# Layer 2's up projection as seven block products instead of eight, with its weights converted early and streamed from DRAM

## The chip, the cores and the metric

The kernel runs on one core of one Trainium2 chip. The metric is device time in microseconds (us). TensorE multiplies matrices into PSUM, VectorE and ScalarE work on SBUF and PSUM, GpSimd (POOL) on SBUF alone, and SyncE (SP) issues all DMA transfers from one queue.

## The reference

Attention with rotary embedding feeds two feed-forward layers. There are 4 x 8 heads of 576 positions by 64; the heads are put side by side, so that a token has 512 features and there are 2304 tokens.

```
x = attention(q, k, v)                     # 2304 x 512
h = x @ w_in;  x = (h - tanh(h)) @ w_out   # layer 1: 512 -> 2048 -> 512
h = x @ w2_in; out = (h * sigmoid(1.702 * h)) @ w2_out   # layer 2, same sizes
```

## The kernel before

Every float32 operand of a matmul is split into a high part (a cast to float32r) and a low part (the remainder), and a product is three matmuls: high by high, high by low, low by high. In the feed-forward layers the tokens lie in six blocks of 384 (`TB`, block number j), and the 2048 hidden features in 16 blocks of 128 (f). An *item* is one pair (j, f). Its `up` (L769, matmuls in `up_chunk`, L716) is 4 blocks of the 512 inputs times three, 12 matmuls of 384 columns. The activation (`act`, L775) follows: in layer 1 four ScalarE and five VectorE steps, in layer 2 a sigmoid on ScalarE (L780) and a product on VectorE (L782). `split` (L808) casts the result to `gh` on ScalarE and subtracts `gl` on GpSimd. `down` (L818) adds to the output: in layer 1 12 matmuls of 384 columns with the weights stationary, in layer 2 9 of 512 columns with the activations stationary. `y_out` (L831) copies the sums out of PSUM and `y_save` stores them, layer 1's to the DRAM tensors `ys`, from which layer 2 fetches its blocks (`x_fetch`, `x_split`). Layer 1 runs blocks 0 and 1 in turns of four f, then the other blocks one by one; layer 2 is 96 items more.

The weights come as 64-bit words. `Conv` loads a block (`load`), and ScalarE, GpSimd and VectorE build float32 numbers (`head`, `bits`), of which `high` and `low` make the two parts. All 16 blocks of a layer stay in SBUF, in slabs of 128 x 4 x 512 (`wpa`, `wpc`, `wpb`). Layer 2's blocks are converted as layer 1's last items free the slabs.

The order on each engine is fixed ahead by `Plan`: each step has a priority, a cost and the tiles that it holds, and the planner picks, engine by engine, the step of the lowest priority number among those that could start about first. Priorities count from a nominal clock, `T(i)`, 4.16 us an item; the planner's own clock may run later than it. PSUM has four named banks (b0 and b1 hold `up` sums, b2 a layer 1 intermediate, b3 a conversion) and four for `down` sums.

Of the kernel before, what the change touches and what calls it, by code (L numbers as in the profile page):

```python
# [21 lines left out]
HP = H // 2  # L22
# [1007 lines left out]
```

## Time and profile before

| | |
|---|---|
| median of 3 runs | 1093.43 us (1093.26 to 1094.11) |
| profiled execution, span from first to last instruction | 1090.6 us |
| what the median has beyond that span | 2.8 us |
| TensorE busy, matmul instructions | 1067.2 us, 6272 |
| VectorE, ScalarE, GpSimd busy | 647.5, 670.1, 597.1 us |

The profiled execution's own time is recorded as that span alone. A matmul's duration overlaps the next one's, so the time between starts, not the duration, is what one more matmul costs.

### The profile page before, as it was taken

To read this page: it belongs to the slowest core of one execution; us is meant where nothing else is said; L and a number is where in the kernel's file an instruction comes from. 1 tells how busy PE (TensorE), PEld (TensorE's weight loads), DVE (VectorE), ACT (ScalarE), POOL (GpSimd) and SP (SyncE) were. 2 spreads that over 40 slices of the span, in tenths; PEclk is the share of its full clock that TensorE was granted. 3 is DMA by queue.
4 is the path that set the end of the run, shared out by engine and by line. 5 is a ranking of instruction groups with operands and counts; after the bars stand their busy time and mean duration, and the time that the engine had idled before them with its cause. 6 is when DMAs were issued, how large, how long until landed. Compare 5 with 4: busy or idle time off the path is not lost.

```text
span 1090.6 us, 17801 instructions
## 1 busy us (share of the span) xinstructions
PE 1067.2 (98%) x6272; PEld 1006.6 (92%) x6272; DVE 647.5 (59%) x1154; ACT 670.1 (61%) x1486; POOL 597.1 (55%) x502
## 2 busy tenths in 40 slices
PE   5999999999999999999999999999999999999998
PEld 4899999998999999999999999999999999999997
DVE  7899999989889987656667589544212111111111
ACT  5999999999887766566575678654322232232322
POOL 2888999986556677254262377767433232332221
PEclk9999999999999999999999999999999999999999
DMA  8777887777523324112031134543101010000000
GB/s 289 276 244 272 286 299 270 258 252 236 154 80 111 105 87 126 34 31 86 2 110 56 44 94 134 157 133 97 59 14 45 1 59 1 16 29 1 30 1 29
DMA packets 80778, 125.64 MB, mean 115 GB/s; under 512 B 9520, under 2 KB 50224, under 8 KB 80688
## 3 DMA queue, kind: packets, MB, share of 16 engines
q1 hardware_dynamic: 80688, 124.49, 34.9%
q8 instruction: 50, 0.82, 0.3%
q14 instruction: 40, 0.33, 0.1%
HBM read 77.20 MB, written 18.95 MB: 88 GB/s over the span
## 4 chain that ended last, share of the span: by engine, by line
PE 80%; DVE 9%; ACT 5%; issue 2%; DMA 2%; POOL 1%; SPq 1%; ACTq 0%; POOLq 0%; DVEq 0%
PE ps_h L716 35%; PE y L829 35%; PE sp L441 4%; PE ps_o L520 3%; PE ps_e L478 2%; DVE mx L447 2%; ACT e L453 2%; DVE el L504 2%; ACT eh L506 1%; DMA qk<-in_qk_dram 1%; DVE cz L289 1%; DVE cz L287 1%; DVE eh L504 1%; PE ps_e L482 1%; POOL qk L364 0%
## 5 line engine op out<-in xcount | busy, mean ns | idle before, releaser
L716 PE MATMUL ps_h<-xh,w 128*128 128x384 f32 x1536 | 422.6, 336 | 0.6 <-DVE xt L529 0.6
L814 POOL TENSOR_TENSOR gl<-t,gh 128x384 fp32r<-128x384 f32 x192 | 194.9, 1016 | 366.6 <-ACT gh L812 358.0
L716 PEld LDWEIGHTS ps_h<-xh,w 128*128 128x128 f32 x1536 | 280.4, 188 | 5.3 <-DVE xt L529 0.8
L716 PE MATMUL ps_h<-xl,w 128*128 128x384 f32 x768 | 257.2, 335 | 0.0
L812 ACT CAST gh<-t 128x384 fp32r<-128x384 f32 x192 | 98.8, 514 | 196.1 <-PE y L829 93.3
L782 DVE TENSOR_TENSOR t<-t,ps_h 128x384 f32<-128x384 f32 x96 | 53.1, 553 | 268.9 <-ACT t L780 268.5
L829 PE MATMUL y<-gh,w 128*128 128x384 f32 x768 | 195.1, 334 | 0.8 <-ACT gh L812 0.8
L829 PE MATMUL y<-w,gh 128*128 128x512 f32 x576 | 179.2, 392 | 0.0
L716 PEld LDWEIGHTS ps_h<-xl,w 128*128 128x128 f32 x768 | 144.2, 188 | 4.1
L780 ACT ACTIVATE t<-ps_h 128x384 f32<-128x384 f32 x96 | 47.2, 492 | 161.8 <-PE ps_h L716 157.1
L829 PEld LDWEIGHTS y<-gh,w 128*128 128x128 f32 x768 | 138.6, 188 | 1.5 <-ACT gh L812 1.5
L829 PE MATMUL y<-gl,w 128*128 128x384 f32 x384 | 128.6, 335 | 1.0 <-POOL gl L814 0.9
L829 PEld LDWEIGHTS y<-w,gh 128*128 128x128 f32 x576 | 106.8, 188 | 17.8
L441 PE MATMUL sp<-kt,qt 128*128 128x288 f32 x624 | 114.3, 311 | 2.0 <-ACT e L453 1.1
L829 PE MATMUL y<-w,gl 128*128 128x512 f32 x288 | 113.9, 396 | 0.0
L453 ACT ACTIVATE e<-sp,mx 128x576 f32<-128x576 f32 x144 | 107.1, 745 | 7.4 <-DVE mx L447 6.3
L447 DVE TENSOR_REDUCE mx<-sp 128x1 f32<-128x576 f32 x144 | 106.6, 747 | 4.0 <-PE sp L441 2.6
L298 POOL TENSOR_TENSOR w<-cz,w 128x512 fp32r<-128x512 f32 x64 | 82.8, 1295 | 46.4 <-ACT w L294 44.7
L506 ACT CAST eh<-ps_e 128x512 fp32r<-128x512 f32 (+2 forms) x208 | 103.3, 527 | 5.3 <-PE ps_e L478 3.4
L504 DVE TENSOR_TENSOR el<-ps_e,eh 128x512 fp32r<-128x512 f32 x144 | 95.8, 684 | 4.9 <-ACT eh L506 3.8
L797 DVE SCALAR_TENSOR_TENSOR w<-z,ps_h 128x384 f32<-128x384 f32 x96 | 52.8, 550 | 76.3 <-ACT t L790 74.7
L441 PEld LDWEIGHTS sp<-kt,qt 128*128 128x128 f32 x624 | 87.9, 189 | 8.9 <-ACT e L453 7.9
(71 smaller groups left out, 1726.3 us busy)
## 6 DMA issues: line engine op xcount, KB each, us to landing
kt<-qk SPq DMA_DIRECT2D x64, 288.0 KB
qk<-in_qk_dram SPq DMA_DIRECT2D x30, 576.0 KB
st<-in_moe_w_in_dram SPq DMA_DIRECT2D x32, 512.0 KB
st<-in_moe_w_out_dram SPq DMA_DIRECT2D x32, 512.0 KB
qt<-qk SPq DMA_DIRECT2D x64, 144.0 KB
x<-xs SPq DMA_DIRECT2D x16, 384.0 KB
v<-in_v_dram SPq DMA_DIRECT2D x16, 320.0 KB
xs<-xt SPq DMA_DIRECT2D x16, 288.0 KB
```

The costliest lines, as they stand in the source:

```text
L298: nc.gpsimd.tensor_sub(w[:, 2 * self.half + 1], self.cz, w[:, 2 * self.half].bitcast(F32))
L441: nc.tensor.matmul(sp[:, half, 0:HS], lhsT=w, rhs=m[:, half * HS:(half + 1) * HS], start=(o == 0), stop=(o == len(ops) - 1))
L447: nc.vector.tensor_reduce(mx, st["sp", n, i], axis=AX.XY, op=ALU.max, negate=True)
L453: nc.scalar.activation(e.rearrange("p (a b) -> p a b", a=2), st.pop(("sp", n, i)), AF.Exp, bias=st.pop(("mx", n, i)), accum_out=st["sum", ...
L504: nc.vector.tensor_sub(lo, src, hi.bitcast(F32))
L506: nc.scalar.copy(hi, src)
L716: nc.tensor.matmul(p, lhsT=wi[:, a, kk, :], rhs=xx[:, kk, :], start=(o == 0), stop=(o == 11))
L782: nc.vector.tensor_mul(gt[i], gt[i], p)
L797: nc.vector.scalar_tensor_tensor(w, z, G_C[3], p, op0=ALU.mult, op1=ALU.mult)
L812: nc.scalar.copy(gs[i][0], g)
L814: nc.gpsimd.tensor_sub(gs[i][1], g, gs[i][0].bitcast(F32))
L829: nc.tensor.matmul(y, lhsT=lhs, rhs=rhs, start=first and o == 0, stop=last and o == 2)
```

## The change

In layer 2, two token blocks (the pair p) and two f blocks (fp and fp + 8) form a *quad*. The four `up` results of a quad are the blocks of a 2 x 2 block product, in which the 512 inputs are halved too. Instead of eight block products of 256 inputs, seven are formed (Strassen's scheme in Winograd's form), each of 6 matmuls of 384 columns, from sums of the weight blocks and of the token blocks. The results share partial sums: ScalarE copies product 1 into a second bank as the start of another sum (`seed`), sets two partial sums aside (`keep`), and VectorE adds them to the last sum (`join`). Seven operand tiles of a token pair are made by GpSimd subtractions and ScalarE casts (`mixed`, `operand`) from the raw blocks. The `down` matmuls are those of before; six sums of a pair stay open over its 8 quads, in the four `down` banks and b2 and b3. `h2` uses b0 and b1.

The weights of layer 2, with the sums of their blocks, are converted while layer 1 runs, split into high and low parts, and stored in DRAM (`w2`). Each quad loads its three slabs again (`w_load`). Layer 1's outputs of blocks 2 to 5 go through the row tiles `rb` and `rc`. In the diff, conversion steps (`word`) are those of `queue` before without `high` and `low`.

```diff
+C2, CU, CL = 34, 6, 25
...
+        if u[0] == "h2":
+            return BANKS[0:2]
+        if u[0] == "y2":
+            return TAGS["y"] + BANKS[2:4]
+        if u[0] == "ws":
+            return SLABS
+        if u[0] == "xo":
+            return ["xh.0", "xl.0", "xh.1", "xl.1"] + SLABS
+        if u[0] == "o":
+            return ["part.0", "part.1", "st.0", "st.1"]
+        if u[0] == "raw":
+            return TAGS["part"] if u[1] else SLABS
+        if u[0] == "yo":
+            return TAGS["rb"] + TAGS["rc"]
+        if u[0] in ALSO:
+            return [x for k in ALSO[u[0]] for x in TAGS[k]]
...
+    ALSO = {"su": ("z", "w"), "g2": ("t",), "g2h": ("gh", "mk"), "g2l": ("gl", "mk")}
+
...
+    SLABS = TAGS["wpa"] + TAGS["wpc"] + TAGS["wpb"]
...
+    w2 = [[dram.tile([128, 4, 512], F32, name=f"w2{s}{i}") for s in range(3)] for i in range(NF // 2)]
...
+    def pieces_of(src, wd, key, dst, reads, urgent, uses):
+        u = ("o",) + key
+
+        def high():
+            if u not in ot:
+                ot[u] = part_tile(u)
+            nc.scalar.copy(ot[u][:, 0:wd].bitcast(F32R), src())
+
+        def low():
+            nc.gpsimd.tensor_sub(ot[u][:, 512:512 + wd].bitcast(F32R), src(), ot[u][:, 0:wd])
+
+        def store():
+            nc.sync.dma_start(out=dst, in_=ot[u][:, 0:1024].rearrange("p (a f) -> p a f", a=2)[:, :, 0:wd])
+
+        f = wd / 512
+        op(urgent, high, [_cost("ACT", 0.23 + 0.38 * f)], reads, [("oh",) + key], [u] + uses)
+        op(urgent, low, [_cost("POOL", 0.18 + 1.12 * f)], reads + [("oh",) + key], [("ol",) + key], [u] + uses)
+        op(urgent, store, [("SP", 0.62, 1.6 * f)], [("oh",) + key, ("ol",) + key], [("w2",) + key], [u], dl=(1.2, 0.8))
+
+    def conv_in(fp, prio, urgent, after):
+        cs = [Conv((1, f), w2_in, w2_out, 0) for f in (fp, fp + NF // 2)]
+        ids = [c.word(prio + n, urgent + n, after) for n, c in enumerate(cs)]
+        cz = [("cz",) + i for i in ids]
...
+        S = [("S", fp, k) for k in range(4)]
+        K = [("in", fp, r) for r in range(4)]
+        pieces_of(lambda: cs[0].cz, 512, K[0], w2[fp][0][:, 0:2], [z[0]], t, cz)
+        pieces_of(lambda: a(1, 1), 256, K[3], w2[fp][1][:, 2].rearrange("p (a f) -> p a f", a=2), [z[1]], t, cz)
+        op(t, lambda: summed(0), cost, [z[1]], [S[0]], cz + [X])
+        op(t, lambda: summed(1), cost, [z[0], S[0]], [S[1]], cz + [X])
+        pieces_of(both, 512, K[1], w2[fp][0][:, 2:4], [S[0], S[1]], t, [X])
+        done = [("ol",) + K[1]]
+        op(t, lambda: summed(2), cost, z + done, [S[2]], cz + [X])
+        op(t, lambda: summed(3), cost, [z[0], S[1]] + done, [S[3]], cz + [X])
+        pieces_of(both, 512, K[2], w2[fp][1][:, 0:2], [S[2], S[3]], t, [X])
+
+    def conv_out(f, prio, urgent, after):
+        c = Conv((1, f), w2_in, w2_out, 1)
...
+        pieces_of(lambda: c.cz, 512, ("out", f), w2[fp][2][:, 2 * n:2 * n + 2], [("z",) + i], urgent + 1, [("cz",) + i])
...
+                P = ("yo", j, d) if j > 1 else ("part", j)
...
+    FP = NF // 2
+    for fp in range(FP):
+        t = T(C2 + CU * fp)
+        conv_in(fp, t, t + CL, t)
+        for n in range(2):
+            u = t + (0.5 + 0.25 * n) * CU * UN
+            conv_out(fp + FP * n, u, u + CL, u)
+
+
+    UQ = 15.7
+    NQ = 3 * FP
+    PROD = {1: (0, 0, 0), 6: (0, 2, 256), 2: (0, 0, 256), 5: (0, 2, 0), 7: (1, 0, 0), 3: (1, 0, 256), 4: (1, 2, 0)}
...
+    def w_load(q, s):
+        t = ws[q, s] = slab(("ws", q, s), "ws")
+        n = 3 if s == 1 else 4
+        nc.sync.dma_start(out=t[:, 0:n].bitcast(F32), in_=w2[q % FP][s][:, 0:n])
...
+    def mixed(p, k):
+        if k in (1, 3, 4):
+            xt2[p, k] = xp.tile([128, 2, TB], F32, tag=cur[0].slot["x", 1, p, k], name="x", bufs=1)
+        if k == 1:
+            nc.gpsimd.tensor_sub(xt2[p, 1], block(p, 0, 1), block(p, 0, 0))
+        elif k == 3:
+            nc.gpsimd.tensor_sub(xt2[p, 3], block(p, 1, 1), block(p, 0, 1))
+        elif k == 2:
+            nc.gpsimd.tensor_sub(block(p, 0, 1), block(p, 1, 1), xt2[p, 1])
+        else:
+            nc.gpsimd.tensor_sub(xt2[p, 4], block(p, 1, 0), block(p, 0, 1))
+
...
+    def operand(p, n, low):
+        a = source(p, n)
+        if not low:
+            xo[p, n] = slab(("xo", p, n), "xo")[:, :, 0:TB]
+            nc.scalar.copy(xo[p, n][:, 0:2], a)
+        else:
+            nc.gpsimd.tensor_sub(xo[p, n][:, 2:4], a, xo[p, n][:, 0:2].bitcast(F32))
+    made = [("w2", "in", fp, r) for fp in range(FP) for r in range(4)] + [("w2", "out", f) for f in range(NF)]
+
+    def x_ops(p):
+        t = T2(FP * p) - (30 if p else 5)
+        R = [("raw", p, h) for h in range(2)]
+        for h in range(2):
+            op(t - 4, lambda h=h: raw_load(p, h), [("SP", 0.62, 1.6)], [("ys", 2 * p + h, d) for d in range(NK)]
+               + ([("h0", FP * p - 5)] if p else made), [("raw", p, h)],
+               [R[h]], t - 14, dl=HBM)
+        X = {k: ("x", 1, p, k) for k in (1, 3, 4)}
+        XO = {n: ("xo", p, n) for n in PROD}
+        held = {1: [R[0]], 2: [R[0]], 3: [R[1]], 4: [X[4]], 5: [X[1]], 6: [R[1]], 7: [X[3]]}
+        got = {1: ("raw", p, 0), 2: ("raw", p, 0), 3: ("raw", p, 1), 4: ("T", p, 4), 5: ("T", p, 1), 6: ("T", p, 2), 7: ("T", p, 3)}
+        add = _cost("POOL", 1.86)
+        for k, reads, uses in ((1, [("raw", p, 0), ("raw", p, 1)], R + [X[1]]),
+                               (3, [("raw", p, 1)], [R[1], X[3]]),
+                               (2, [("T", p, 1), ("T", p, 3), ("raw", p, 1)], [R[1], X[1]]),
+                               (4, [("T", p, 2), ("raw", p, 0)], R + [X[4]])):
+            op(t + k * 0.01, lambda k=k: mixed(p, k), [add], reads, [("T", p, k)], uses)
+        for o, n in enumerate((1, 6, 2, 5, 7, 3, 4)):
+            for low in (False, True):
+                op(t + 2 * o, lambda n=n, low=low: operand(p, n, low), [add if low else _cost("ACT", 0.8)],
+                   [got[n]] + ([("xoh", p, n)] if low else []), [("xol" if low else "xoh", p, n)], held[n] + [XO[n]])
+
+    def product(q, n):
+        p = q // FP
+        s, a, o = PROD[n]
+        w, x = ws[q, s], xo[p, n]
+
...
+        b = {1: 0, 2: 0, 6: 1, 5: 1, 3: 1, 7: 2, 4: 2}[n]
+        if n in (1, 7):
+            hq[q, b] = bank(("h2", q, b), "ps_h")[:, 0:TB]
+        c = 0
+        for k in range(2):
+            for lw, lx in ((0, 0), (0, 1), (1, 0)):
+                nc.tensor.matmul(hq[q, b], lhsT=wt(lw, k), rhs=x[:, 2 * lx + k], start=n in (1, 7) and c == 0,
+                                 stop=n in (2, 3, 4) and c == 5, skip_group_check=True)
+                c += 1
+
+    def seed(q):
+        hq[q, 1] = bank(("h2", q, 1), "ps_h")[:, 0:TB]
+        nc.scalar.copy(hq[q, 1], hq[q, 0])
+
+    def keep(q, n):
+        su[q, n] = slab(("su", q, n), "su", F32)
+        nc.scalar.copy(su[q, n], hq[q, 1])
+
+    def join(q, n):
+        if n == 0:
+            su[q, 3] = slab(("su", q, 3), "su", F32)
+            nc.vector.tensor_add(su[q, 3], hq[q, 2], su[q, 4])
+        else:
+            nc.vector.tensor_add(hq[q, 2], hq[q, 2], su[q, 2])
+
...
+    def quad_ops(q):
+        p, fp = divmod(q, FP)
+        t = T2(q)
+        H = [("h2", q, b) for b in range(3)]
+        Ws = [("ws", q, s) for s in range(3)]
+        SU = {n: ("su", q, n) for n in (2, 3, 4)}
+        for s in range(3):
+            src = [("w2", "in", fp, 2 * s + r) for r in range(2)] if s < 2 else [("w2", "out", f) for f in (fp, fp + FP)]
+            op(t - 20 + 2 * s, lambda s=s: w_load(q, s), [("SP", 0.62, 4.0)], src + ([("h0", q - 2)] if q > 2 else []),
+               [("wsl", q, s)], [Ws[s]], t - 34, dl=HBM)
+
+        def pr(n, prio, reads, writes, b):
+            op(t + prio, lambda: product(q, n), [("PE", 1.04, 1.21)],
+               [("xoh", p, n), ("xol", p, n), ("wsl", q, PROD[n][0])] + reads, writes, [H[b], Ws[PROD[n][0]], ("xo", p, n)])
+
+        pr(1, 0, [("h2", q - 1)] if q else [], [("h0", q)], 0)
+        op(t + 1, lambda: seed(q), [_cost("ACT", 0.5)], [("h0", q)], [("h1", q)], [H[0], H[1]])
+        pr(2, 2, [], [("h0", q)], 0)
+        pr(6, 2.1, [], [("h1", q)], 1)
+        op(t + 3, lambda: keep(q, 2), [_cost("ACT", 0.5)], [("h1", q)], [("k2", q)], [H[1], SU[2]])
+        pr(5, 5, [], [("h1", q)], 1)
+        op(t + 6, lambda: keep(q, 4), [_cost("ACT", 0.5)], [("h1", q)], [("k4", q)], [H[1], SU[4]])
+        pr(3, 8, [], [("h1", q)], 1)
+        pr(7, 9, [], [("h2", q)], 2)
+        op(t + 10, lambda: join(q, 0), [_cost("DVE", 0.555)], [("h2", q), ("k4", q)], [("c3", q)], [H[2], SU[3], SU[4]])
+        op(t + 10, lambda: join(q, 1), [_cost("DVE", 0.555)], [("k2", q), ("c3", q)], [("h2", q)], [H[2], SU[2]])
+        pr(4, 12, [], [("h2", q)], 2)
+        for u, at, src, hold in ((0, 3, ("h0", q), H[0]), (1, 9, ("h1", q), H[1]), (3, 11, ("c3", q), SU[3]), (2, 13, ("h2", q), H[2])):
+            G, GH, GL = ("g2", q, u), ("g2h", q, u), ("g2l", q, u)
+            op(t + at, lambda u=u: act2(q, u, 0), [_cost("ACT", 0.62)], [src], [("a2", q, u)], [hold, G])
+            op(t + at + 1, lambda u=u: act2(q, u, 1), [_cost("DVE", 0.555)], [src, ("a2", q, u)], [("g", q, u)], [hold, G])
+            op(t + at + 2, lambda u=u: split2(q, u, 0), [_cost("ACT", 0.515)], [("g", q, u)], [("gh2", q, u)], [G, GH, GL])
+            op(t + at + 2, lambda u=u: split2(q, u, 1), [_cost("POOL", 1.01)], [("g", q, u), ("gh2", q, u)], [("gl2", q, u)], [G, GH, GL])
+            n, j = divmod(u, 2)
+            for c in range(3):
+                Y = ("y2", p, j, c)
+                op(t + at + 6 + c, lambda u=u, c=c: down2(q, u, c), [("PE", 0.693, 0.9)],
+                   [("gh2", q, u), ("gl2", q, u), ("wsl", q, 2)], [("yd2", p, j, c)], [GH, GL, Ws[2], Y])
...
+    for q in range(NQ):
+        if q % FP == 0:
+            x_ops(q // FP)
+        quad_ops(q)
```

## Rows read from the trace of the kernel before

**Rows 1.** The page: busy time by engine; granted clock and DMA rate in 40 slices.

```profile
PE 1067.2 (98%) x6272; PEld 1006.6 (92%) x6272; DVE 647.5 (59%) x1154; ACT 670.1 (61%) x1486; POOL 597.1 (55%) x502
...
PEclk9999999999999999999999999999999999999999
...
GB/s 289 276 244 272 286 299 270 258 252 236 154 80 111 105 87 126 34 31 86 2 110 56 44 94 134 157 133 97 59 14 45 1 59 1 16 29 1 30 1 29
```

**Rows 2.** The chain that ended last, layer 2: start us, us, what.

```profile
691.47 2.08 PE y L829 x9
...
1003.34 2.10 PE ps_h L716 x12
1005.45 2.08 PE y L829 x9
...
1080.81 6.18 PE y L829 x27
```

**Rows 3.** Stretches: length, busy us of PE, PEld, DVE, ACT, POOL, clock, DMA.

```profile
270.00:290.00 20.00, 18.79 (x128) 17.61 (x127) 17.42 (x32) 15.84 (x38) 8.46 (x10) 1.00 0.62 183
...
640.00:680.00 40.00, 40.00 (x232) 40.00 (x232) 37.26 (x67) 31.01 (x66) 26.57 (x27) 1.00 0.40 122
...
389.00:660.00 271.00, 270.17 (x1554) 268.92 (x1554) 189.29 (x355) 172.80 (x375) 133.86 (x135) 1.00 0.23 70
```

**Rows 4.** Timeline near the end: the last `up` matmul of an item, its sigmoid, its product.

```profile
1076.29 0.33 PE L716 MATMUL ps_h<-xh,w 128*128 128x384 f32 x1
...
1076.72 0.49 ACT L780 ACTIVATE t<-ps_h 128x384 f32<-128x384 f32 x1 [1.88 <-PE ps_h L716]
...
1077.24 0.55 DVE L782 TENSOR_TENSOR t<-t,ps_h 128x384 f32<-128x384 f32 x1 [3.63 <-ACT t L780]
```

**Rows 5.** Timeline of layer 1: a cast on ScalarE and the `down` that waited for it.

```profile
371.78 0.51 ACT L812 CAST gh<-t 128x384 fp32r<-128x384 f32 x1 [1.90 <-DVE t L805]
...
372.35 0.62 PE L829 MATMUL y<-gh,w 128*128 128x384 f32 x2 [0.48 <-ACT gh L812]
```

**Rows 6.** Groups by line and form: busy us, mean ns of one, then idle before.

```profile
L814 POOL TENSOR_TENSOR gl<-t,gh 128x384 fp32r<-128x384 f32 x192 | 194.9, 1016 | 366.6 <-ACT gh L812 358.0 <-ACT z L788 3.5 <-issue 2.6
...
L812 ACT CAST gh<-t 128x384 fp32r<-128x384 f32 x192 | 98.8, 514 | 196.1 <-PE y L829 93.3 <-DVE t L805 80.1 <-PE ps_h L716 17.4
...
L298 POOL TENSOR_TENSOR w<-cz,w 128x512 fp32r<-128x512 f32 x64 | 82.8, 1295 | 46.4 <-ACT w L294 44.7 <-DVE el L504 0.9 <-PE y L829 0.4
...
L364 POOL TENSOR_TENSOR qk<-qk,tab 128x1152 f32<-128x1152 f32 x28 | 74.4, 2668 | 5.9 <-PE ps_o L520 2.8 <-DMA xs<-xt 2.1 <-DMA st<-in_moe_w_out_dram 0.4
...
L782 DVE TENSOR_TENSOR t<-t,ps_h 128x384 f32<-128x384 f32 x96 | 53.1, 553 | 268.9 <-ACT t L780 268.5
...
L780 ACT ACTIVATE t<-ps_h 128x384 f32<-128x384 f32 x96 | 47.2, 492 | 161.8 <-PE ps_h L716 157.1 <-POOL gl L814 4.7
...
L287 DVE SCALAR_TENSOR_TENSOR cz<-cp,cz 128x512 int32<-128x512 int32 x64 | 43.7, 683 | 40.7 <-POOL cz L285 37.5 <-ACT cp L276 2.8
L285 POOL TENSOR_SCALAR cz<-st 128x512 int32<-128x512 uint8 x64 | 42.1, 658 | 5.5 <-DMA st<-in_moe_w_out_dram 0.2
...
L276 ACT ACTIVATE cp<-st 128x512 f32<-128x512 f32 x64 | 40.5, 632 | 0.0
...
L294 ACT CAST w<-cz 128x512 fp32r<-128x512 f32 x64 | 39.5, 620 | 12.3 <-DVE cz L289 11.6
...
L426 POOL TENSOR_TENSOR vw<-v,vw 128x640 fp32r<-128x640 f32 x16 | 25.5, 1593 | 4.9 <-PE sp L441 2.3 <-ACT vw L370 2.0
...
L370 ACT CAST qk<-qk 128x1152 fp32r<-128x1152 f32 x15 | 17.5, 1167 | 0.0
...
L838 ACT COPY part<-y 128x384 f32<-128x384 f32 x24 | 10.6, 482 | 0.2
...
L370 ACT CAST vw<-v 128x640 fp32r<-128x640 f32 x7 | 5.5, 792 | 0.0
```

**Rows 7.** Timeline of SP's queue at the end of layer 1.

```profile
688.87 1.91 SPq L846 DMA_DIRECT2D ys<-part  x4
```

More of the change, by code (lines that the diff above doesn't have):

```diff
@@ L806, in act, with split @@
             gt[i] = t
[L808 removed]
+    def split(i, k, names=("gh", "gl")):
         g = gt[i]
         if k == 0:
[L811 removed]
+            key = (i,) if isinstance(i, int) else i
+            gs[i] = [slab((t,) + key, t[-2:]) for t in names]
             nc.scalar.copy(gs[i][0], g)
@@ L842, in y_save @@
     def y_save(i, d):
-        mo, j = items[i][:2]
-        n = (TB, DM)[mo]
-        r = j * TB + d * 128
-        nc.sync.dma_start(out=out[r:r + 128, :] if mo else ys[j][d], in_=part[mo, j][:, d * n:(d + 1) * n])
+        j = items[i][0]
+        nc.sync.dma_start(out=ys[j][d], in_=part[j, d])
     UN = 4.16
@@ L915, in item_ops @@
+        for d in range(NK):
+            Y = ("y", d, j, lo_of[i])
+            w = 3 * 0.173
+            op(t + MD + 0.01 * d, lambda d=d: down(i, d), [("PE", w, w + 0.2)],
+               [("gh", i), ("gl", i)] + [(x, 0, f, 1) for x in ("wh", "wl")]
+               + (["down"] if i or d else []), [("yd", d, j, lo_of[i]), "down"], [GH, GL, Wt, Y])
             if last:
-                n = (TB, DM)[mo]
-                P = ("part", mo, j)
-                cost = _cost("ACT", 0.49 if n == TB else 0.59) if lo_of[i] == 0 else _cost("DVE", 0.547 if n == TB else 0.68)
@@ L936, in attention_moe_kernel @@
         item_ops(i)
-    for f in range(NF):
-        for half in range(2):
-            m = 2 * f + half
-            t = T(n1 - 10 + m if m < 10 else n1 + (m - 10) / 2)
-            Conv((1, f), w2_in, w2_out, half).queue(t - 6, t, max(0, t - 30))
-    for i in range(n1, 2 * n1):
-        for (mo, j), s in first_item.items():
-            if mo and s - 8 == i or (mo == 1 and i == n1 and s < n1 + 8):
-                fetch_ops(mo, j, T(s - 8))
-        item_ops(i)
+    FP = NF // 2
[5 more added lines that the diff above has]
+            conv_out(fp + FP * n, u, u + CL, u)
@@ new lines, in split2, with down2 @@
+    def split2(q, u, k):
+        g = gt[q, u]
+        if k == 0:
+            gs[q, u] = [slab((t, q, u), t[1:] if 0 else t) for t in ("g2h", "g2l")]
+            nc.scalar.copy(gs[q, u][0], g)
+        else:
+            nc.gpsimd.tensor_sub(gs[q, u][1], g, gs[q, u][0].bitcast(F32))
+    def down2(q, u, c):
+        p, fp = divmod(q, FP)
+        n, j = divmod(u, 2)
+        gh, gl = gs[q, u]
+        cols = slice(c * 128, (c + 1) * 128)
+        first, last = fp == 0 and n == 0, fp == FP - 1 and n == 1
+        if first:
+            acc["2", p, j, c] = bank(("y2", p, j, c), "y")
+        y = acc["2", p, j, c]
+        for o, (a, g) in enumerate(((0, gh), (1, gh), (0, gl))):
+            nc.tensor.matmul(y, lhsT=g[:, cols], rhs=ws[q, 2][:, 2 * n + a, :], start=first and o == 0, stop=last and o == 2)
```

296 lines of the change are left out of this document (174 added, 122 removed).

## Prediction

> **What bounds the kernel now.** I read the page first: TensorE is busy 98% of the span and its granted clock never falls, while DMA traffic in the second half is a small part of what the first half shows possible [rows 1]. "Busy" can hide waits, so next comes the chain of work that ended last: in layer 2 it is TensorE alone, 12 matmuls of `up` in 2.10 us, then 9 of `down` in 2.08 us, and again, and the end is three groups of `down` in a row [rows 2]. Then the stretches: in the second half of layer 1 (389 to 660 us) TensorE is busy 270.2 of 271 us, and even where the old conversions of layer 2's weights fill VectorE to 93% (640 to 680 us) TensorE loses nothing [rows 3]. So from there on the time is the number of matmuls times their pitch. Removing a matmul pays in full as long as no new wait takes its place; moving work off the other engines pays nothing by itself. The profiled execution has a span of 1090.6 us; the median of the runs is 1093.43, so about 2.8 us lie around the span, and I take them as unchanged.
>
> **What is removed.** Layer 2's `up` is 96 items of 12 matmuls, 1152. After the change it is 24 quads (two token blocks by two f blocks) of seven products of 6 matmuls, 1008. The `down` matmuls stay at 24 x 36 = 864, the same form. So 144 matmuls of 384 columns go. At the pitch of the row, 2.10/12 = 0.175 us, that is **-25.2 us**, or 1.05 us per quad [rows 2]. A quad then holds 42 x 0.175 + 36 x 2.08/9 = 7.35 + 8.32 = 15.67 us of TensorE.
>
> The Trainium skill ("TensorE: Matmul & The Clock Gate", section "Back-to-back issue gap") gives an isolated warm matmul of N columns N/2.4 + 2.5 ns, here 162.5 ns, by which 144 matmuls would be worth 23.4 us (an estimate from that page). The rows have 175 ns with the weight loads in between, and the measurement decides.
>
> **The new order inside a quad.** Before, an `up` only needed a free bank. Now TensorE's seven products depend on other engines, with two banks for three sums. The hops, from the rows: ScalarE starts 0.43 us after the last matmul of an `up` starts, which is 0.26 us after the slot in which the next matmul could start [rows 4]; a ScalarE copy of 128x384 out of PSUM takes 0.48 [rows 6]; TensorE starts 0.06 after ScalarE ends [rows 5]. So:
> - product 1 to `seed` to products 2 and 6: product 2 adds into the bank that `seed` reads, so it waits too, 0.26 + 0.48 + 0.06 = 0.80 us. The bank that `seed` writes comes free by the quad before: its product 4, then sigmoid, multiply and the copy, 0.26 + 0.49 + 0.03 + 0.55 + 0.03 + 0.48 + 0.06 = 1.90 us, of which the new product 1 covers 1.05. So 0.85 us at most are left.
> - product 6 to `keep` to product 5, and product 5 to `keep` to product 3: 0.80 us each.
> - product 7 to two `join` on VectorE (0.55 each, 0.03 between) to product 4: 0.26 + 1.13 + 0.06 = 1.45 us [rows 4, 6].
>
> Behind a waiting `seed` or `keep` on ScalarE stand sigmoids and `gh` casts, for which later `down` groups wait. What `down` work must cover is 0.85 + 0.80 + 0.80 + 1.45 = 3.9 us, and a quad has 12 groups of three `down` matmuls, 0.69 us each, 8.3 us. The groups are also ready in time: a block needs 0.26 + 0.49 + 0.55 + 0.51 + 1.02 and hops, about 3.1 us, from its last product to its `gl` [rows 4, 6], and three blocks of the quad before are waiting while this quad's chain runs. The closest fit is product 5 to product 3, where the priorities leave one group (0.69) against 0.80. Lower bound 0 per quad; upper bound 3.9, all hops bare. I take 0.15 us per quad, the one tight hop and a little queueing on ScalarE: **+3.6 us**. The other engines have room: per quad ScalarE 3 x 0.48 + 4 x (0.49 + 0.51), with an eighth of seven 768-wide copies (about 0.89, between the 640 and 1152 rows) and of six output copies, about 6.7 of 15.67 us; VectorE 6 x 0.55 = 3.3; GpSimd 4 x 1.02 and an eighth of eleven 768-wide subtractions of about 1.86 (between the 640 and 1152 rows), 6.6 us [rows 6].
>
> **The streamed weights.** A quad loads 1.05 + 0.79 + 1.05 = 2.88 MB in 15.67 us, 184 GB/s; the page has slices of 299 GB/s [rows 1], at which it takes 9.6 us. SP issues them in one queue with the x loads and the output stores, each waiting for a free slab; a load that waits holds up those behind it. Twenty slots serve: two operand sets of seven and one raw block fill 15 at the worst, around a change of token pair, and leave five. A set of three for the next quad can then go only as the last quad's slabs come free, about 20, 16 and 9 us before each is read. I cost it at nothing, hidden by that lead; if the lead is gone, 9.6 us at each of the two pair changes.
>
> **The conversions.** They leave the stretch where they cost TensorE nothing, so that gains nothing. They arrive in layer 1, by their load times from about 389 us. 32 words need VectorE 32 x 2 x 0.68, 44 us, as before; ScalarE 32 x 0.63 + 40 x 0.62 + 8 narrow copies, 48 us; GpSimd 32 x 0.66 + 40 x 1.30 + 40 of 256 columns at about 0.74 (extended from the 384 and 512 rows), 103 us, where it was 63 [rows 6]. Added to what 389 to 660 us already holds, an over-count since some old conversions lie in it, VectorE comes to 233, ScalarE 221 and GpSimd 236 of 271 us [rows 3]. That is full but under what 640 to 680 shows without loss. What can hurt is one conversion step ahead of a `gl` or an activation in an engine's queue, 0.6 to 1.3 us; TensorE then waits for `gl`. Lower bound 0 (640 to 680); upper bound the 270 to 290 stretch, 1.21 us lost of 20, which over 271 us is 16 us [rows 3]. I take **+1.5 us**, near the row of the same stage. The outputs of blocks 2 to 5 now share three row tiles, so the fourth copy waits for the first store; the four stores issue in 1.91 us [rows 7] and the next block's `down` needs that bank more than 4 us later, so nothing.
>
> **Opening of layer 2 and end.** The two raw x loads of the first pair wait for every stored piece, and then eleven 768-wide GpSimd steps (20.5 us, some 27 beside the `gl` steps) make the operands. The first nine `down` matmuls in layer 2's form start at 691.5 us, two items behind their `up` [rows 2], so layer 2 starts near 691.5 - 2.1 - 8.3 = 681 us; even conversions that end at 650 leave the first operands in time. Opening, pair changes and the tail together: **+0.8 us** (lower 0).
>
> Sum: 1090.6 - 25.2 + 3.6 + 1.5 + 0.8 = 1071.3 us of span, with 2.8 around it **1074 us**.
>
> **Rivals.**
> 1. The full gain: all hops and conversions hidden, 1068 to 1070. For it: the cover counts above. Against: the one tight hop and fuller queues. 0.14.
> 2. A jam in layer 1: conversions in front of `gl`. For: three engines above 80%, GpSimd with 40 us more. Against: 640 to 680. At the upper bound 1093.4 - 25.2 + 3.6 + 16.4 + 0.8 = 1089. 0.10.
> 3. Late data: the stores end only with layer 1, then loads of 1.6 MB (5.3 us) and 20.5 us of GpSimd against some 10 us of TensorE's work, 16 us lost, or slabs late at the pair changes, 19 us. 1088 to 1091. 0.10.
> 4. Slower: the hops inside a quad stay bare, because the fixed order puts `down` groups elsewhere or the other engines lag it. It decides at 1.05 us per quad, 27% of the 3.9 us; all bare gives 24 x 3.9 = 94 us, 1162. For: before, no matmul of `up` waited for a copy. Against: 8.3 us of cover for 3.9. 0.09, and 0.03 for other losses beyond 25 us.
> 5. No difference: losses happen to equal the gain, 0.04.
>
> The forecast, 1070 to 1079, has 0.50. **Numbers.** Faster by over 0.2% (2.2 us, about what a measurement of this kernel can tell from no change) 0.50 + 0.14 + 0.20 = 0.84; within 0.04; slower 0.12. The range from 1068 to 1089 leaves out the slower cases, the equal one and a little of rivals 1 to 3; the forecast's own range is 1070 to 1079.
>
> **What will show it.** Right: layer 2's stretch is about 376 + 4 us long and TensorE waits in it are a few tenths per quad, on product 3; layer 1 ends within 2 us of before. Wrong: waits on `keep`, `join` or `seed` above 1 us per quad (rival 4); waits of `down` on `gl` between 389 and 660 (2); a gap of TensorE near 681 us or at each eighth quad, ended by a DMA or by GpSimd's operand step (3).

## Result, and the profile after

The changed kernel takes **1076.87 us** (median of 4 runs, 1075.84 to 1079.64). The kernel before, run beside it, took 1093.35 us. That is 16.5 us less; the forecast was 1074 us, 19.3 us less. The recorded ratio is 0.9856 [0.9842, 0.9870]; it is not the quotient of the two medians, which is 0.9849 and lies inside the interval. The profiled execution took 1075.84 us with a span of 1074.0 us.

On the page, TensorE has 144 instructions fewer, and the granted clock does not fall. GpSimd has 74 us more to do, and the last part of the DMA row, almost empty in [rows 1], now carries the stream.

```profile
PE 1048.0 (98%) x6128; PEld 980.6 (91%) x6128; DVE 673.4 (63%) x1196; ACT 715.7 (67%) x1571; POOL 671.1 (62%) x559
...
PEclk9999999999999999999999999999999999999999
...
GB/s 284 279 239 295 262 274 315 241 264 247 158 100 91 106 97 210 185 175 206 208 201 239 174 301 314 83 378 118 69 150 338 191 209 132 215 347 251 108 1 59
```

**Where the 16.6 us of span went.** Two points divide both executions: the slot in which layer 1's own matmuls are done, and the end of the last `down`. In the kernel before, layer 1's last `down` and the `up` that follows it in TensorE's timeline are these:

```profile
689.05 0.33 PE L829 MATMUL y<-gl,w 128*128 128x384 f32 x1
689.23 0.33 PE L716 MATMUL ps_h<-xh,w 128*128 128x384 f32 x1
```

By 689.23 TensorE had already done two `up` items of layer 2 (24 matmuls, the second from 685.07 to 687.15, 2.08 us each). Without them layer 1 would have ended at 689.23 - 4.16 = 685.07. In the kernel after, 18 product matmuls, the first two rows, stand between layer 1's last `down` groups (L1119 is a product, L929 a `down` of layer 1; the last row is cut off where the view ends):

```profile
685.58 1.20 PE L1119 MATMUL ps_h<-xo,ws 128*128 128x384 f32 x6
...
688.70 2.24 PE L1119 MATMUL ps_h<-xo,ws 128*128 128x384 f32 x12
...
692.69 0.33 PE L929 MATMUL y<-gl,w 128*128 128x384 f32 x1
692.86 1.37 PE L1119 MATMUL ps_h<-xo,ws 128*128 128x384 f32 x7
```

Their slots are 1.04 and 2.08 us, so layer 1 would have ended at 692.86 - 3.12 = 689.74. The last 27 `down` matmuls close both chains, at 1080.81 + 6.18 before [rows 2] and here:

```profile
1064.02 6.17 PE y L1164 x27
```

| part | before | after | difference | forecast |
|---|---|---|---|---|
| attention, up to layer 1's first `up` | 286.31 | 286.60 | +0.3 | 0 |
| layer 1, to the points above | 398.8 | 403.1 | +4.4 | +1.5 |
| layer 2, to the end of the last `down` | 401.9 | 380.5 | -21.5 | -25.2 + 3.6 + 0.8 = -20.8 |
| last output copy and stores | 3.6 | 3.8 | +0.2 | in the 0.8 |
| span | 1090.6 | 1074.0 | -16.6 | -19.3 |

**A quad.** TensorE's products in the timeline, from product 5 of one quad to product 5 of the next. The pitch is 882.23 - 866.36 = 15.87 us; the working had 15.67 + 0.15 + a little.

```profile
866.36 1.23 PE L1119 MATMUL ps_h<-xo,ws 128*128 128x384 f32 x6
867.43 0.63 PE L1164 MATMUL y<-ws,g2h 128*128 128x512 f32 x2
867.89 0.40 PE L1164 MATMUL y<-ws,g2l 128*128 128x512 f32 x1
868.16 2.38 PE L1119 MATMUL ps_h<-xo,ws 128*128 128x384 f32 x12
...
882.23 1.23 PE L1119 MATMUL ps_h<-xo,ws 128*128 128x384 f32 x6
```

Product 5 (866.36) is followed by one `down` group, then by products 3 and 7 together. In between, ScalarE takes the copy `keep`, and its row in ScalarE's timeline ends at 868.10, 0.06 us before product 3 starts:

```profile
867.62 0.48 ACT L1129 COPY su<-ps_h 128x384 f32<-128x384 f32 x1 [2.94 <-PE ps_h L1119]
```

The weight loads' waits between 690 and 1074 us name this copy and, but for one `g2l` of 0.2 us, nothing else (us in total, times, longest):

```profile
PEld ps_h L1119 <- ACT su L1129: 6.8, 22, 0.3
```

**Layer 1.** The stretches that answer to [rows 3]. From 270 to 290 us, in attention, TensorE is busy 18.79 of 20 us as before. From 389 to 660 us VectorE has 27 us more, ScalarE 30, GpSimd 81, and TensorE is busy 2.85 us less:

```profile
389.00:660.00 271.00, 267.32 (x1527) 263.99 (x1527) 216.33 (x397) 202.36 (x430) 214.64 (x226) 1.00 0.63 212
```

It has also done 27 matmuls fewer there (1527 against 1554), which at 2.08/12 us each is 4.7 us. So a wait costs more than its idle time; the first matmul behind the wait at 590 us (last row of the second view below) takes 0.44 us instead of 0.33.

TensorE's largest waits within layer 1 (from 690 us on its matmuls show none):

```profile
PE y L929 <- POOL gl L916: 1.6, 4, 0.5
PE y L929 <- ACT yo L941: 1.3, 1, 1.3
PE ps_h L826 <- DVE t L900: 0.9, 2, 0.7
```

The third line is a conversion standing in an engine's queue. The rows of VectorE and of the matmul at 590 us: two conversion steps (L320, L322) go ahead of the activation (L898, L900), which ends at 590.08, and the bank comes free for TensorE then.

```profile
587.73 0.69 DVE L320 SCALAR_TENSOR_TENSOR cz<-cp,cz 128x512 int32<-128x512 int32 x1 [1.13 <-POOL cz L318]
588.46 0.69 DVE L322 SCALAR_TENSOR_TENSOR cz<-cp,cz 128x512 int32<-128x512 int32 x1
589.07 0.55 DVE L898 SCALAR_TENSOR_TENSOR w<-z,ps_h 128x384 f32<-128x384 f32 x1
589.53 0.55 DVE L900 TENSOR_TENSOR t<-ps_h,t 128x384 f32<-128x384 f32 x1
...
590.13 0.44 PE L826 MATMUL ps_h<-xh,w 128*128 128x384 f32 x1 [0.70 <-DVE t L900]
```

The second is an output block with three row tiles: three copies go at once, the fourth starts 6.6 us after them, and TensorE needs its bank. The stores of the first three tiles were issued by 627.2 us. From 627.2 us to the fourth copy ScalarE works through ten other steps, four of them conversion steps, with one gap of 0.26 us; so when the copy ran was set by the order on ScalarE at least as much as by the tile.

```profile
624.26 1.52 ACT L941 COPY yo<-y 128x384 f32<-128x384 f32 x3
...
632.41 0.47 ACT L941 COPY yo<-y 128x384 f32<-128x384 f32 x1
...
632.93 0.61 PE L929 MATMUL y<-gh,w 128*128 128x384 f32 x2 [1.29 <-ACT yo L941]
```

### The profile page after: what moved, and what is told of

It reads as the page before. It is cut to its first block, busy times and chain, and to the rows that moved or that the text cites. A ratio compares the mean times of both kernels' runs of the same rounds, so it can differ in the third digit from the quotient of the medians.

```text
span 1074.0 us, 17841 instructions
## 1 busy us (share of the span) xinstructions
PE 1048.0 (98%) x6128; PEld 980.6 (91%) x6128; DVE 673.4 (63%) x1196; ACT 715.7 (67%) x1571; POOL 671.1 (62%) x559
## 4 chain that ended last, share of the span: by engine, by line
PE 64%; DVE 14%; ACT 9%; POOL 5%; issue 4%; DMA 2%; SPq 1%; ACTq 0%; DVEq 0%; POOLq 0%
PE y L1164 19%; PE ps_h L1119 17%; PE y L929 9%; PE ps_h L826 9%; PE sp L551 4%; PE ps_o L630 3%; PE ps_e L588 2%; ACT e L563 2%; DVE mx L557 2%; DVE t L906 2%; DVE u L904 2%; ACT eh L616 2%; DVE el L614 1%; DVE u L902 1%; DVE cz L322 1%
## 5 line engine op out<-in xcount | busy, mean ns | idle before, releaser
L1152 POOL TENSOR_TENSOR g2l<-t,g2h 128x384 fp32r<-128x384 f32 x96 | 97.4, 1016 | 226.1 <-ACT g2h L1150 226.0
L1144 DVE TENSOR_TENSOR t<-t,ps_h 128x384 f32<-128x384 f32 x72 | 39.8, 553 | 273.6 <-ACT t L1142 269.1
L826 PE MATMUL ps_h<-xh,w 128*128 128x384 f32 x768 | 209.6, 335 | 1.4 <-DVE t L900 0.9
L1119 PE MATMUL ps_h<-xo,ws 128*128 128x384 f32 x1008 | 198.8, 340 | 0.0
L929 PE MATMUL y<-gh,w 128*128 128x384 f32 x768 | 195.2, 335 | 1.8 <-ACT yo L941 1.3
L1119 PEld LDWEIGHTS ps_h<-xo,ws 128*128 128x128 f32 x1008 | 178.5, 188 | 14.8 <-ACT su L1129 6.8
L1164 PE MATMUL y<-ws,g2h 128*128 128x512 f32 x576 | 179.2, 392 | 0.0
L826 PEld LDWEIGHTS ps_h<-xh,w 128*128 128x128 f32 x768 | 139.9, 188 | 2.8 <-DVE t L900 1.8
L929 PEld LDWEIGHTS y<-gh,w 128*128 128x128 f32 x768 | 138.6, 188 | 2.8 <-ACT yo L941 1.6
L916 POOL TENSOR_TENSOR gl<-t,gh 128x384 fp32r<-128x384 f32 x96 | 97.7, 1019 | 60.9 <-ACT gh L914 49.2
L929 PE MATMUL y<-gl,w 128*128 128x384 f32 x384 | 129.0, 336 | 1.6 <-POOL gl L916 1.6
L826 PE MATMUL ps_h<-xl,w 128*128 128x384 f32 x384 | 128.3, 334 | 0.0
L1164 PEld LDWEIGHTS y<-ws,g2h 128*128 128x128 f32 x576 | 106.8, 188 | 15.8
L1164 PE MATMUL y<-ws,g2l 128*128 128x512 f32 x288 | 113.9, 395 | 0.0
```

The source lines that it names most:

```text
L826: nc.tensor.matmul(p, lhsT=wi[:, a, kk, :], rhs=xx[:, kk, :], start=(o == 0), stop=(o == 11))
L916: nc.gpsimd.tensor_sub(gs[i][1], g, gs[i][0].bitcast(F32))
L929: nc.tensor.matmul(y, lhsT=w[:, a, cols], rhs=g, start=first and o == 0, stop=last and o == 2)
L1119: nc.tensor.matmul(hq[q, b], lhsT=wt(lw, k), rhs=x[:, 2 * lx + k], start=n in (1, 7) and c == 0, stop=n in (2, 3, 4) and c == 5, skip_grou ...
L1152: nc.gpsimd.tensor_sub(gs[q, u][1], g, gs[q, u][0].bitcast(F32))
L1164: nc.tensor.matmul(y, lhsT=g[:, cols], rhs=ws[q, 2][:, 2 * n + a, :], start=first and o == 0, stop=last and o == 2)
```

## Experiments

Theory A says that layer 2 is bound by the number of matmuls, that its one remaining loss is the hop product 5, `keep`, product 3, and that layer 1's loss comes from the conversions and from the row tiles. The rivals stand in the expectations. Each kernel was run beside the kernel before (1093.49, 1093.50 and 1093.09 us in the three groups). All edits are to the changed kernel.

| kernel | median us | ratio to the kernel before |
|---|---|---|
| changed kernel | 1076.87 | 0.9856 [0.9842, 0.9870] |
| product 7 ahead of product 3 | 1072.81 | 0.9809 [0.9796, 0.9823] |
| one f block pair converted | 1071.01 | 0.9793 [0.9779, 0.9806] |
| eight products | 1101.43 | 1.0075 [1.0059, 1.0091] |
| each `keep` twice | 1087.81 | 0.9946 [0.9933, 0.9960] |
| each weight load twice | 1210.57 | 1.1076 [1.1059, 1.1093] |
| 7 ahead of 3, and the x tiles for outputs | 1073.82 | 0.9826 [0.9813, 0.9840] |
| the same, conversions planned later | 1092.41 | 0.9992 [0.9983, 1.0000] |
| the same as two rows above, conversions spread wider | 1099.85 | 1.0057 [1.0044, 1.0069] |
| conversions later, first x loads not held | 1070.54 | 0.9794 [0.9780, 0.9807] |
| the same with three row tiles | 1071.99 | 0.9807 [0.9793, 0.9820] |
| 7 ahead of 3, each `keep` twice | 1075.12 | 0.9833 [0.9820, 0.9847] |

**1. Product 7 ahead of product 3.**

```diff
+        pr(7, 7.8, [], [("h2", q)], 2)
         pr(3, 8, [], [("h1", q)], 1)
-        pr(7, 9, [], [("h2", q)], 2)
```

> Product 7 stands ahead of product 3 in each quad; nothing else changes. Theory A (what layer 2 loses per quad is the bare end of the hop product 5, keep, product 3, covered by one group of down of 0.69 us): with product 7 (1.05 us) in the hop too, the stall of about 0.15 us per quad goes, the quad's pitch falls from 15.87 to about 15.72 us, and the time falls by about 3.6 us, to a ratio of about 0.982 against the kernel before. Rival B (the loss is the streamed weights, or the changing between the two forms of matmul): pitch 15.87 and ratio 0.9856 as they were.

4.1 us less. TensorE's timeline of the same place: the twelve matmuls of products 7 and 3 now follow without the gap (2.26 instead of 2.38), and the next product 5 starts 15.72 us after this one (its row is cut off where the view ends, so it counts five of the six matmuls).

```profile
867.54 1.23 PE L1119 MATMUL ps_h<-xo,ws 128*128 128x384 f32 x6
...
869.31 2.26 PE L1119 MATMUL ps_h<-xo,ws 128*128 128x384 f32 x12
...
883.26 1.05 PE L1119 MATMUL ps_h<-xo,ws 128*128 128x384 f32 x5
```

0.15 us x 24 = 3.6 us. Theory A holds: product 7 fills another bank and covers the rest of the copy. (The profiled execution is the slowest of the five, 1075.04 us: its attention is 2.5 us longer. So the pitch is read here, and not the span.)

**2. Few conversions.**

```diff
-    for fp in range(FP):
+    for fp in range(1):
         t = T(C2 + CU * fp)
...
-        nc.sync.dma_start(out=t[:, 0:n].bitcast(F32), in_=w2[q % FP][s][:, 0:n])
+        nc.sync.dma_start(out=t[:, 0:n].bitcast(F32), in_=w2[0][s][:, 0:n])
...
```

> Only the first of the eight f pairs of layer 2 is converted and stored, and every quad loads that pair's slabs; seven eighths of the conversions are left out, the loads and the matmuls are all there. Theory A (layer 1 loses about 4 us to conversion steps queued ahead of its own steps and of the output copies): TensorE's loss between 389 and 660 us falls from 3.7 us to the 0.8 of the kernel before, and the time falls by about 3 us, ratio about 0.983. Rival B (layer 1's loss comes from the three shared row tiles of the outputs alone): the wait of down on the output copy near 631 us stays, 1.3 us and more, and the time falls by no more than 2.5 us.

5.9 us less than the changed kernel, where 3 were expected; between the two profiled executions it is 4.8 us. In the stretch from 389 to 660 us TensorE is back at 270.18, as before the change [rows 3]:

```profile
389.00:660.00 271.00, 270.18 (x1554) 268.79 (x1553) 183.68 (x347) 169.26 (x367) 135.92 (x134) 1.00 0.28 89
```

The wait for the output copy is gone too, though the row tiles are still three: the fourth copy of that block now starts at 627.53 us instead of 632.41. So all of layer 1's 4.4 us comes with the conversions, and rival B, that the three row tiles cost it by themselves, fell.

**3. Eight products.** Product 6 is computed twice into its sum.

```diff
-        for k in range(2):
+        for k in (0, 1, 0, 1) if n == 6 else range(2):
```

> Product 6 is issued twice in each quad (its six matmuls again, so that one sum is wrong), which gives an eighth product's matmuls in the same scheme. Theory A (layer 2 is bound by the number of its matmuls): each quad grows by 6 x 0.175 = 1.05 us, the time by 25 us to about 1102 us, ratio about 1.008: all of the gain is the seventh eighth. Rival B (the quad is bound by its hops or by the stream of weights): the added matmuls fill waits and cost less than half of that, under 1089 us.

24.6 us more. Product 5 with its `down` group, then products 3 and 7, come every 881.11 - 864.21 = 16.90 us, 1.03 us more for six matmuls:

```profile
864.21 2.37 PE L1119 MATMUL ps_h<-xo,ws 128*128 128x384 f32 x12
...
881.11 2.37 PE L1119 MATMUL ps_h<-xo,ws 128*128 128x384 f32 x12
```

So the time of layer 2 is the number of its matmuls, in the new form as well, and the term -25.2 is measured from the other side as 24.6. With eight products the new form is 8 us slower than the kernel before: by the sizes above those are the hop's 3.6 and layer 1's 4.4, which nothing pays for then.

**4. Each `keep` twice**, which makes both `keep` hops about 0.5 us longer.

```diff
         nc.scalar.copy(su[q, n], hq[q, 1])
+        nc.scalar.copy(su[q, n], hq[q, 1])
```

> Each keep is done twice, so that the two hops over ScalarE through keep are 0.37 to 0.48 us longer; the order of the matmuls is as it was. Theory A: the hop from product 6 to product 5 has four groups of down (2.8 us) in it and costs nothing more; the hop from product 5 to product 3 has one and is bare by the whole of the addition: 0.37 to 0.48 us per quad, 9 to 11.5 us in all, ratio about 0.995. Rival B (hops are covered with room to spare): no change.

10.9 us more than the changed kernel, 0.46 per quad. TensorE's waits from 690 us on, and one of them in its timeline:

```profile
PE ps_h L1119 <- ACT su L1130: 8.4, 22, 0.4
```

```profile
874.43 2.35 PE L1119 MATMUL ps_h<-xo,ws 128*128 128x384 f32 x12 [0.38 <-ACT su L1130]
```

Only the group of twelve (products 3 and 7) waits. The other hop, product 6 to product 5, took its half microsecond without a loss, so it has at least that much cover to spare.

**5. Each `keep` twice with product 7 ahead**, the edits of 1 and 4 together.

> Each keep done twice, as in the earlier run, but with product 7 ahead of product 3. Theory A (the price of a keep is only what its hop lacks in cover): the hop now has a group of down and product 7 in it, 1.74 us against 0.80 + 0.48 = 1.28, so doubling costs nothing: ratio 0.981, pitch 15.72. Rival B (ScalarE's added work itself costs, wherever it stands): the 10 us of the earlier run again, ratio about 0.990.

2.3 us more than with the exchange alone, where the same copies cost 10.9 without it. In the quads the doubled copy costs nothing, as theory A has it; product 5 comes every 15.72 us again, and the twelve matmuls keep their 2.26 us:

```profile
866.60 1.23 PE L1119 MATMUL ps_h<-xo,ws 128*128 128x384 f32 x6
...
868.36 2.26 PE L1119 MATMUL ps_h<-xo,ws 128*128 128x384 f32 x12
...
882.32 1.23 PE L1119 MATMUL ps_h<-xo,ws 128*128 128x384 f32 x6
```

Part of the 2.3 us stands at the opening of layer 2, where no `down` covers the hops yet: 18 product matmuls in a row take 3.76 us there, against 3.28 in kernel 1. The rest is not accounted for, and the intervals of experiments 1 and 5 overlap.

**6. Each weight load twice.**

```diff
-        nc.sync.dma_start(out=t[:, 0:n].bitcast(F32), in_=w2[q % FP][s][:, 0:n])
+        for _ in range(2):
+            nc.sync.dma_start(out=t[:, 0:n].bitcast(F32), in_=w2[q % FP][s][:, 0:n])
```

> Every slab of layer 2 is loaded twice, one load after the other into the same tile: 5.77 MB per quad. Theory A (the stream hides, with time to spare, up to the rate that DMA reaches): at 15.87 us a quad the need is 363 GB/s, above the 299 GB/s of the best slice before but under the 378 of the best slice after the change, so it costs somewhere from 0 to (5770/299 - 15.87) x 24 = 82 us; the loads of a lead of a quad or more should keep it in the lower half. Rival B (the stream as it stands is already close to setting the pace): every quad grows to at least 19 us, 75 us and more in all.

134 us more, beyond what theory A named and, by its size, in rival B's range. Stretches of layer 2 (columns as in [rows 3]) and TensorE's waits after 690 us:

```profile
700.00:860.00 160.00, 144.51 (x704) 128.86 (x704) 33.73 (x57) 62.34 (x122) 66.58 (x53) 0.95 0.73 267
860.00:1020.00 160.00, 120.39 (x545) 104.20 (x545) 24.17 (x42) 42.44 (x84) 48.04 (x39) 0.88 0.74 273
```

```profile
PE ps_h L1120 <- DMA ws<-w: 39.3, 11, 6.5
PE ps_h L1120 <- ACT su L1130: 34.8, 2, 23.1
```

The two waits for `keep` (second row) stand where the operands of the next token pair are made: ScalarE's first casts wait 13.08 and 27.10 us there for the x loads (`part<-ys`), and `keep` stands behind them.

The doubled stream ran at 267 to 273 GB/s. A quad then needs 5.77 MB / 270 = 21.4 us, and 24 x (21.4 - 15.87) = 133 us, about what was lost. But that is not the most that this queue moves: the changed kernel's page above has a slice of 378 GB/s. The second load of a slab goes into the tile that the first one fills, so SP holds it until the first has landed. In the whole run that is 72 waits, one for each doubled load; in the changed kernel SP waits for something else, for TensorE to free the slabs. The two rows, this run's first:

```profile
SPq L1046 <- DMA ws<-w: 468.9, 72, 10.3
SPq L1045 <- PE ps_h L1119: 234.8, 34, 41.0
```

So the experiment does not decide between theory A and rival B: it lengthens the stream by bytes and by waits together. That the single stream has time to spare is read from the changed kernel itself: no wait of TensorE for a `ws` load stands in its trace, and SP's loads wait for slabs. Even at 270 GB/s it would take 10.7 of 15.87 us, so about 5 us per quad are to spare; this is an estimate, on the low side, since that rate holds the added waits.

**7. The x tiles for output copies.** The outputs of blocks 2 to 5 may use free x tiles besides the three row tiles; product 7 stays ahead.

```diff
-            return TAGS["rb"] + TAGS["rc"]
+            return TAGS["rb"] + TAGS["rc"] + TAGS["x"]
...
```

> With product 7 ahead of product 3; and layer 1's outputs of blocks 2 to 5 may use the two x tiles too, five tiles for four copies. Theory A (of the 4.4 us that layer 1 lost, 1.5 is the fourth copy waiting for a row tile at one block's end, the rest single conversion steps in the way): 1.5 us less than with the swap alone, ratio about 0.9795. Rival B (the order of ScalarE, not the tile, sets when that copy runs): no change, 0.981.

No gain: 1073.82 against 1072.81. The wait for `yo` is gone from TensorE's list, and others stand there:

```profile
PE ps_h L826 <- DVE t L902: 2.0, 4, 0.9
PE y L931 <- POOL gl L918: 1.1, 3, 0.5
```

Theory A fell here, and rival B, that ScalarE's order and not the tile sets when the copy runs, fits. The order of the engines is planned anew, and the loss comes out at another place. With experiment 2 this shows that the row tiles were where the loss appeared once, not what made it.

**8 and 9. Conversions later, or wider.** Both start from kernel 7. Kernel 8 gives a piece's conversion steps priority numbers 45 us behind its load's on the nominal clock instead of 25 (the 20 in the expectation are microseconds of that clock, about five items). Kernel 9 gives each pair of f blocks 8 items of layer 1 instead of 6, from item 30 on.

```diff
-C2, CU, CL = 34, 6, 25
+C2, CU, CL = 34, 6, 45
```

```diff
-C2, CU, CL = 34, 6, 25
+C2, CU, CL = 30, 8, 25
```

> As the run with five output tiles, and the conversion steps stand 20 items further back in priority (CL from 25 to 45), so that fewer of them go ahead of layer 1's own steps. Theory A: layer 1 loses nothing more than before (0.8 us of 389 to 660), 4.4 us less than the swap alone, unless the first operands of layer 2 come late: ratio 0.977. Rival B (what layer 1 loses is set by how full the engines are, not by which step goes first): no more than the five tiles gave, 0.9795; Rival C: the opening of layer 2 waits for the conversions, and the gain is given back there, 0.981 or more.

> As the run with five output tiles, with the conversions spread over eight items per pair of f blocks instead of six, starting four items earlier (C2 30, CU 8). Theory A: as with the lower priority, layer 1's loss goes and the ratio is about 0.977. Rival B (the early start meets layer 1's own conversions, which fill VectorE to 90% up to 400 us): layer 1 loses more before 410 us, ratio 0.980 or more.

Kernel 8 lost what the change had gained, as its rival C said, and kernel 9 is 6.4 us slower than the kernel before. In 8, the stretch in layer 1 is better (TensorE 269.45 of 271, against 267.32), but behind it TensorE does 155 matmuls from 660 to 690 us, where the changed kernel does 175, and then the opening of layer 2 stands still, with a mean granted clock of 0.56:

```profile
389.00:660.00 271.00, 269.45 (x1545) 267.31 (x1544) 216.38 (x398) 198.85 (x426) 207.18 (x219) 1.00 0.62 209
690.00:720.00 30.00, 18.46 (x58) 15.14 (x58) 2.69 (x5) 12.05 (x20) 22.30 (x14) 0.56 0.52 184
```

SP's queue, and ScalarE's and GpSimd's first operand steps, show why. The raw x loads go out right behind the last stored piece, at 676.76 instead of 653.65; ScalarE comes to the first cast at 690.62, behind layer 1's output copies, and GpSimd's chain starts at 691.53, where in the changed kernel it started at 669.88.

```profile
676.35 0.32 SPq L374 DMA_DIRECT2D w<-part  x1
676.76 1.33 SPq L1052 DMA_DIRECT2D raw<-ys  x2
```

```profile
690.62 1.56 ACT L1077 CAST xo<-raw 128x768 fp32r<-128x768 f32 x2
```

```profile
691.53 3.59 POOL L1079 TENSOR_TENSOR xo<-raw,xo 128x768 fp32r<-128x768 f32 x2 [3.40 <-ACT xo L1077]
```

TensorE then waits 5.03 and 3.85 us for operands, and from 689 to 716 us its matmuls take about twice the time, 5 of them 1.97 us:

```profile
703.23 0.69 PE L1121 MATMUL ps_h<-xo,ws 128*128 128x384 f32 x1 [5.03 <-ACT xo L1077]
707.77 1.97 PE L1121 MATMUL ps_h<-xo,ws 128*128 128x384 f32 x5 [3.85 <-POOL xo L1079]
```

Kernel 9 lost in the same place: its raw x loads go out at 694.19, again right behind the last stored piece, and TensorE waits 9.8 and 6.5 us for `xo`. Its two theories had looked elsewhere.

**10 and 11. The first x loads not held.** In 10, kernel 8 with the raw loads of the first pair ordered after layer 1's outputs alone and not after every stored piece. In 11, the same without the x tiles.

```diff
-               + ([("h0", FP * p - 5)] if p else made), [("raw", p, h)],
+               + ([("h0", FP * p - 5)] if p else []), [("raw", p, h)],
```

> As the run with conversions further back (CL 45, five output tiles, product 7 ahead of product 3), but the raw x loads of the first pair no longer wait until every piece of the weights is stored; the slab loads still wait for their own pieces. Theory A (that run lost its gain because this one wait put the operands' making behind the last conversion, TensorE then stood still for some 10 us and ran the next 12 us at half its clock): the opening closes up, layer 1 stays without added loss, and the time is about 4 us under the swap alone, ratio about 0.977. Rival B (with the conversions that late, GpSimd cannot make the operands in time whatever waits for what): the opening still loses 5 us or more, ratio 0.982 to 0.999.

> The same without the two extra output tiles. Theory A (with the conversions out of the way the fourth output copy waits for no one, as when seven eighths of them were left out): the same time as with the five tiles, ratio about 0.977. Rival B (the tiles themselves cost about 1.5 us per bad block): 1.5 to 4 us more.

That one edit takes 8 from 1092.41 to 1070.54 us: the wait for every stored piece alone had cost 22 us, and rival B of kernel 10 fell. The operand waits are gone, and TensorE works through the opening at full clock:

```profile
690.00:720.00 30.00, 30.00 (x152) 27.27 (x152) 6.33 (x12) 11.76 (x25) 10.14 (x11) 1.00 0.94 353
```

Kernel 10 is 22.6 us faster than the kernel before and 6.3 faster than the changed one. The intervals of kernels 1, 10 and 11 overlap, so its gains of 2.3 us over kernel 1, where theory A had 4, and of 1.5 over kernel 11 are not certain. Whether the x tiles matter is left open.

## Why the prediction was right, point by point

- **TensorE bounds the kernel; removed matmuls pay in full.** Right. Layer 2 became 21.5 us shorter, and six matmuls more per quad cost 24.6 us (experiment 3). The term -25.2 stands: with the hop's 3.6 taken out, layer 2 lost 25.1. The estimate of 23.4 by the isolated gap that the Trainium skill gives ("TensorE: Matmul & The Clock Gate", section "Back-to-back issue gap") is further from both measurements.
- **The hops: 0.15 us per quad, one tight hop.** Right in place and size. The hop named is the one that waits; its removal gave 0.15 per quad (experiment 1), and 0.48 more there costs 0.46 (experiment 4). The remaining hops, 3.1 of the 3.9 us, are covered. Rival 4, that they stay bare, is refuted with it.
- **The streamed weights at nothing.** Right: TensorE never waits for a slab, and SP waits for slabs to come free. The 9.6 us of the working, by 299 GB/s from one slice, are neither confirmed nor refuted by experiment 6, whose 267 to 273 GB/s hold the waits that it added.
- **The conversions: +1.5 us, by the row of 640 to 680.** Wrong in size: 4.4 us, within its bounds of 0 to 16. This is the term that makes the prediction 2.7 us too low in span, and the prediction's own sign, layer 1 ending within 2 us of before, did not hold. The loads were well estimated (VectorE 216 measured for 233, ScalarE 202 for 221, GpSimd 215 for 236), and the mechanism was as written, a conversion step ahead of an activation or a `gl`. The reading of the row was wrong: "full but under what 640 to 680 shows" is true of VectorE alone. In that row VectorE is busy 93%, ScalarE 78 and GpSimd 66 [rows 3]; the sums of the working are 86, 82 and 87% of 271 us. So the row could not bound what the other two would do. That a higher load by itself makes the loss is not shown, and kernel 10 speaks against it: from 389 to 690 us ScalarE and GpSimd are busy 225.3 and 239.7 us there, against 222.6 and 235.8 in the changed kernel, but TensorE loses 2.3 us instead of 3.7. Where the steps stand in the order counts too.
- **Three row tiles, "so nothing".** A wait of 1.3 us did appear there. Experiments 2 and 7 show that it belongs to the term above: with few conversions it goes, and more tiles don't bring the time back.
- **Opening, "even conversions that end at 650 leave the first operands in time".** Right as the kernel stands (stores of the last pieces issued by 653.6 us, no wait of TensorE at 685). Of the +0.8 about 0.3 was there: 0.2 at the end, and 0.1 in layer 2 beyond the terms above. But rival 3 was nearer than its 0.10 made it look: with the last piece stored at 676 it comes true at about 20 us (experiment 8), and its cause is the one condition that all pieces be stored (experiment 10). The working named that condition, and rival 3 priced it at 16 us.

Outside the terms, the median is 2.87 us above the profiled span, as the 2.8 of the working had it; that this came so close is partly luck, for the four runs lie 3.8 us apart. What stays open: which of layer 1's conversion steps could be placed so that the rest of the 4.4 us goes. In kernel 10 TensorE is busy 269.35 of the 271 us from 389 on, but 29.32 of the 30 us behind them, where the changed kernel loses nothing; so 1.3 us of it come back.

## What to carry to other kernels

Where one engine is busy to the end, price a change by the instructions it removes from that engine, then go through each new hop between engines and compare its length with the work that is put in between; only the uncovered part counts, and exchanging two independent steps can supply it. Work moved off a stretch where it was free is not free elsewhere: compare the load of each engine in whose queue it will stand, and what will stand behind it there, not only the stage. A wait on "everything is done" should be cut down to what the next step reads, since it turns a small delay far ahead into a stall.

## What the runs showed of the hardware that was not expected

The working had 0.55 us for every VectorE step of 128x384. The multiply of `act2` (L1144) that reads both inputs from SBUF takes that long only when GpSimd does nothing beside it. In the changed kernel 22 of the 24 take 0.93 to 0.95 us, each with half a microsecond of a GpSimd step beside it, and one 1.42 with 1.04 us beside it; the one with none beside it takes 0.55. In kernel 1, whose order puts most of them where GpSimd is idle, those without a GpSimd step beside them take 0.56. The multiplies with one input in PSUM take 0.54 to 0.56 in all of both runs. First the changed kernel, then kernel 1:

```profile
1061.63 1.02 POOL L1152 TENSOR_TENSOR g2l<-t,g2h 128x384 fp32r<-128x384 f32 x1 [5.51 <-ACT g2h L1150]
1062.13 0.94 DVE L1144 TENSOR_TENSOR t<-t,su 128x384 f32<-128x384 f32 x1 [0.18 <-ACT t L1142]
...
1060.44 0.56 DVE L1144 TENSOR_TENSOR t<-t,su 128x384 f32<-128x384 f32 x1 [0.18 <-ACT t L1142]
```

It is off the path here.

A stall can cost more than its own length. In kernel 8 TensorE stood still for 1.00 and 0.80 us behind layer 1's last `gh` and `gl`, up to 688.2 us. The granted clock is 0.74 from 688 to 690 us, 0.50 from 690 to 716, which is the lower of TensorE's two levels (1.2 of 2.4 GHz), and 0.94 from 716 to 718. So it had fallen before the waits of 5.03 and 3.85 us for operands, and stayed low through them: the 18 matmuls from 710.31 us on came every 0.33 us, where at the full clock it is 0.175.
